# Moving the transposed activations out of the weight ring, with two changes to the start: one core, forgetting attention followed by spectral mixing

## The chip, the cores and the metric

The kernel runs on one core of one Trainium2 chip. The metric is the device time of one execution in microseconds (us), the median of several runs.

A word on two clocks. A run's reported time is 1.7 us longer than the span of the trace of that same run (489.44 against 487.7 us before the change). Times inside a trace count from the start of its span. "Mode" below means the matrix product for one Fourier mode; a "tile" is the 1 MB slot that holds the weights of four modes for one quarter of the input channels (0.5 MB real, 0.5 MB imaginary part, loaded as two DMAs).

In the profile lines PE is TensorE, PEld its weight loads, DVE VectorE, ACT ScalarE and POOL GpSimd; L83 is line 83 of that kernel, and `x6` means six instructions in one row.

## The reference, cut to what matters

```python
# q, k, v: (8, 8, 576, 64); f: (8, 8, 576); w_r, w_i: (64, 512, 512); w_ch: (512, 512)
attn = softmax(q @ k^T / 8 + cum[i] - cum[j], causal) ; x = attn @ v      # cum = cumsum(log f)
x = x.transpose(0, 2, 1, 3).reshape(8, 576, 512)
X = rfft(x, axis=1)[:, :64]
Y = einsum('bmd,mde->bme', X, w_r + 1j * w_i)          # 64 modes, 134 MB of float32 weights
y = irfft(Y, n=576, axis=1)
u = x + y
out = u + maximum(u @ w_ch, 0)
```

## The kernel before

The weights are cast to bfloat16 by the DMA on their way (67.64 MB landed through its queue, w_ch included, for 134 MB of float32) and stream through a ring of 9 slots. They are needed in order: 64 tiles, 16 for each quarter `dc` of the input channels. Attention runs in 32 steps (quarter by batch), and from step 9 on each step also does two tiles of modes for the quarter before it. When attention is over, 16 tiles are left; with them go the projections of x (`emit_xw`, which needs x^T) and of y (`emit_y`). A last stage adds all up and stores.

```python
    wpool = ctx.enter_context(tc.tile_pool(name="wpool", bufs=NRING))     # NRING = 9
    ...
    def emit_w_load(n):
        dc, g = tile_of(n)
        wb = wpool.tile([128, 2, MG, D], BF16, tag="wb", name="wb")
        for t, src in enumerate((moe_w_r, moe_w_i)):
            nc.gpsimd.dma_start(wb[:, t, :, :], ...)
    ...
        emit_basis()                  # Fourier basis, part of the setup
        emit_transposes(0)            # the first attention step's casts and transposes
        for s in range(NS + 1):
            ...
    # in emit_transposes(s):
            early = 5 <= s < B
            (nc.gpsimd if early else nc.vector).tensor_tensor(vb, v, wdec6, ALU.mult)
    ...
        XW = bsb.tile([128, B, NSB, D], BF16, name="XW")
        yy = bsb.tile([128, B, 2, D], BF16, name="yy")
    ...
            def emit_xw(b):
                xT = wpool.tile([128, NDC, SP], BF16, tag="wb", name="xT")   # a ring slot
                for eb in range(NDC):
                    ...                                   # 5 transposes into ptr
                    nc.vector.tensor_copy(xT[:, eb, :], ptr[:, :])
                for sb in range(NSB):
                    ...                                   # 4 matmuls with wch into pxw
                    nc.scalar.copy(XW[:, b, sb, :], pxw[:, :])
            ...
            while nmode < last:
                emit_modes(nmode)
                nmode += 1
                if nmode <= last - GL:                    # last = 64, GL = 4
                    if nx < B:
                        emit_xw(nx)
                        nx += 1
                    next_w()
                ...                                       # emit_y between the last four tiles
```

The order on each engine is not the order of this text: a scheduler decides it when the program is built.

The softmax here doesn't subtract the row's maximum and nothing guards it: scores larger than these inputs give would overflow.

## Time and profile before

| | before |
|---|---|
| time, median of 3 runs | 487.81 us (487.59 to 488.44) |
| HBM traffic | 163.73 MB read, 9.44 MB written |
| TensorE / VectorE / ScalarE / GpSimd busy | 68% / 52% / 51% / 27% of the span |
| first mode matmul | 89.7 us |
| projections of x | 381.1 to 428.0 us |
| end of the last mode, last stage | 444.4 us, then 43.3 us |

Four rows of the page's 40 slices (12.2 us each; busy tenths, TensorE's granted clock in tenths, GB/s moved), and the head of the chain that ended last, as shares of the span. This chain is the last instruction, followed back at each step to what it had waited for; a q marks an engine's sequencer, and "issue" is time without a visible cause:

```profile
PE   0668477899548566565566677763322899998994
PEclk9979789999875657766755677885555699989999
DMA  8999999999999999999999999999999999630577
GB/s 206 268 268 264 235 262 268 216 261 264 261 243 210 232 235 235 235 235 235 235 235 226 234 207 207 206 206 207 206 206 206 207 206 159 96 54 1 194 301 282
DMA 54%; PE 22%; ACT 7%; issue 2%; DVE 2%; POOL 0%; POOLq 0%; ACTq 0%; DVEq 0%
```

DMA is full for 33 slices and then fades (159, 96, 54 GB/s), while TensorE, which had idled (3, 3, 2, 2), is suddenly full. The two have changed places: first TensorE waits for weights, then weights wait for TensorE. GpSimd's timeline, which holds the weight issues, says why (start, duration, and in brackets the idle time before and what ended it):

```profile
399.58 0.74 POOL L83 DMA_DIRECT2D wb<-in_moe_w_r_dram  x1 [9.60 <-PE ptr L558]
400.31 0.76 POOL L83 DMA_DIRECT2D wb<-in_moe_w_i_dram  x1
410.65 0.74 POOL L83 DMA_DIRECT2D wb<-in_moe_w_r_dram  x1 [9.59 <-PE ptr L558]
411.38 0.75 POOL L83 DMA_DIRECT2D wb<-in_moe_w_i_dram  x1
422.39 0.74 POOL L83 DMA_DIRECT2D wb<-in_moe_w_r_dram  x1 [10.26 <-PE A L102]
```

Until 384 us a tile was issued every 5.1 us; here one in 11 us, after waits of some 10 us for the transposes (`ptr`): the slot that the load needs comes free only when TensorE gets on. The stretches of time show both sides, and an earlier hole. Each line has the stretch and its length, then the busy us (and number of instructions) of PE, PEld, DVE, ACT and POOL, then TensorE's clock, the busy share of DMA (1.24 is full when only weights move) and GB/s:

```profile
90.00:92.00 2.00, 1.97 (x58) 1.89 (x57) 2.00 (x7) 2.00 (x3) 0.16 (x1) 1.00 0.56 159
92.00:94.00 2.00, 1.75 (x47) 1.39 (x44) 1.42 (x6) 2.00 (x5) 1.41 (x3) 1.00 0.61 163
...
350.00:370.00 20.00, 4.75 (x128) 4.03 (x128) 2.43 (x4) 0.00 (x0) 5.92 (x8) 0.50 1.24 206
370.00:390.00 20.00, 11.37 (x109) 6.09 (x110) 4.29 (x10) 2.83 (x5) 5.92 (x8) 0.59 1.24 207
...
415.00:420.00 5.00, 5.00 (x40) 2.71 (x38) 1.69 (x4) 2.51 (x5) 0.00 (x0) 1.00 0.78 129
420.00:425.00 5.00, 4.99 (x65) 3.08 (x64) 2.21 (x5) 1.50 (x4) 1.48 (x2) 1.00 0.23 21
425.00:430.00 5.00, 5.00 (x100) 3.46 (x99) 1.01 (x2) 2.82 (x5) 0.00 (x0) 1.00 1.17 191
```

At 350 to 370 us TensorE works 4.75 of 20 us at half clock; at 420 to 425 us DMA runs at 0.23 where 1.24 is full. The hole at 90 us is the moment when the ring's first nine tiles had landed and no slot was free yet: no part of a weight load lands between 89.3 and 96.5 us.

In the start, one wait of TensorE stands out in its timeline:

```profile
58.68 0.66 PE L367 MATMUL tp<-ident_bf,vb 96*128 96x96 bf16 x6 [5.70 <-POOL vb L358]
```

GpSimd's scaling of v for steps 5 to 7 stands in its queue behind weight issues that wait for earlier loads, and TensorE stands still for 5.7 us.

### The profile page before, as it was taken

The numbers are of one execution on the slowest core, as the hardware profiler recorded it, in microseconds if no ns is written. First come the engines' busy times: TensorE is split into PE (matmuls) and PEld (weight loads), VectorE is DVE, ScalarE is ACT, GpSimd is POOL, SyncE is SP. The second block draws the span as 40 slices with busy tenths as digits, with TensorE's granted clock in tenths as the row PEclk, the third lists the DMA queues.
The fourth block names the chain that finished last, engine by engine and source line by source line (L and its number), as shares of the span: only waits on it lengthen the run. The fifth ranks groups of instructions, "written<-read, shape, count | busy, mean of one in ns | idle before, by whom it ended". The sixth has DMA issues, their size and how long they took to land.

```text
span 487.7 us, 11410 instructions
## 1 busy us (share of the span) xinstructions
PE 329.6 (68%) x4842; PEld 238.2 (49%) x4842; DVE 251.6 (52%) x618; ACT 250.0 (51%) x372; POOL 130.1 (27%) x157
## 2 busy tenths in 40 slices
PE   0668477899548566565566677763322899998994
PEld 0456355778446454454454555552311455565441
DVE  4858388898544444444444456552010322345874
ACT  2769589999545444444444556540000255434663
POOL 6111400241122122222221233223223311100795
PEclk9979789999875657766755677885555699989999
DMA  8999999999999999999999999999999999630577
GB/s 206 268 268 264 235 262 268 216 261 264 261 243 210 232 235 235 235 235 235 235 235 226 234 207 207 206 206 207 206 206 206 207 206 159 96 54 1 194 301 282
DMA packets 93203, 106.27 MB, mean 218 GB/s; under 512 B 4000, under 2 KB 88480, under 8 KB 93152
## 3 DMA queue, kind: packets, MB, share of 16 engines
q0 software_dynamic: 68112, 67.64, 83.4%
q1 hardware_dynamic: 25040, 37.90, 24.2%
q8 instruction: 38, 0.62, 0.5%
q14 instruction: 13, 0.11, 0.1%
HBM read 163.73 MB, written 9.44 MB: 355 GB/s over the span
## 4 chain that ended last, share of the span: by engine, by line
DMA 54%; PE 22%; ACT 7%; issue 2%; DVE 2%; POOL 0%; POOLq 0%; ACTq 0%; DVEq 0%
DMA wb<-in_moe_w_i_dram 42%; DMA wb<-in_moe_w_r_dram 12%; PE pxw L567 8%; PE A L102 2%; ACT E_129 L429 2%; PE pu L658 2%; PE pyw L579 2%; PE ptr L558 2%; PE pz L662 2%; PE pz L666 1%; ACT E_128 L429 1%; PE ps L422 1%; PE tp L367 1%; PE pav L456 1%; PE pu L654 1%
## 5 line engine op out<-in xcount | busy, mean ns | idle before, releaser
L102 PEld LDWEIGHTS <-wb 128*128 128x128 bf16 x2048 | 68.3, 101 | 123.4 <-DMA wb<-in_moe_w_i_dram 98.0
L83 POOL DMA_DIRECT2D wb<-in_moe_w_r_dram x64 | 47.7, 745 | 213.7 <-DMA wb<-in_moe_w_r_dram 92.9
L83 POOL DMA_DIRECT2D wb<-in_moe_w_i_dram x64 | 47.7, 746 | 105.4 <-DMA wb<-in_moe_w_i_dram 105.4
L429 ACT ACTIVATE E_129<-ps 128x1024 bf16<-128x1024 f32 x64 | 54.4, 869 | 15.2 <-PE ps L422 13.2
L429 ACT ACTIVATE E_128<-ps 128x1024 bf16<-128x1024 f32 x64 | 54.2, 871 | 6.8 <-PE ps L422 6.3
L574 ACT CAST XW<-pxw 128x512 bf16<-128x512 f32 x40 | 22.6, 586 | 66.9 <-PE pxw L567 66.9
L102 PE MATMUL A<-XT_1366,wb 128*128 128x16 bf16 x512 | 21.5, 175 | 38.0 <-DMA wb<-in_moe_w_i_dram 33.9
L113 DVE TENSOR_TENSOR Yacc<-A,Yacc 128x256 f32<-128x256 f32 x32 | 14.1, 441 | 62.9 <-PE A L102 62.2
L102 PE MATMUL A<-XT_2871,wb 128*128 128x16 bf16 x512 | 20.4, 174 | 29.8 <-DMA wb<-in_moe_w_i_dram 27.8
L567 PE MATMUL pxw<-wch,xT 128*128 128x512 bf16 x160 | 39.3, 400 | 0.0
L677 POOL TENSOR_TENSOR uo<-uo 128x1024 f32<-128x1024 f32 (+1 forms) x16 | 28.6, 1810 | 30.7 <-ACT uo L676 27.9
L102 PE MATMUL A<-XT_4376,wb 128*128 128x16 bf16 x512 | 16.4, 172 | 28.1 <-DMA wb<-in_moe_w_i_dram 17.7
L465 DVE TENSOR_TENSOR x_all<-pav,rcp 128x384 bf16<-128x384 f32 x64 | 31.1, 486 | 0.5
L422 PE MATMUL ps<-QTs,KTz_0_124 128*128 128x512 bf16 (+2 forms) x96 | 28.0, 337 | 2.7 <-ACT E_129 L429 1.7
L376 ACT COPY KTz_0_124<-tp 64x576 bf16<-64x576 bf16 x16 | 10.7, 667 | 36.6 <-PE tp L367 36.6
L422 PE MATMUL ps<-QTs,KTz_0_126 128*128 128x512 bf16 (+2 forms) x96 | 27.0, 337 | 3.6 <-ACT E_128 L429 2.2
L117 DVE TENSOR_TENSOR YT<-A,Yacc 128x256 bf16<-128x256 f32 x12 | 7.3, 611 | 42.0 <-PE A L102 42.0
L456 PE MATMUL pav<-va,E_128 128*128 128x65 bf16 x480 | 27.6, 217 | 1.4 <-DVE va L402 1.3
L376 ACT COPY KTz_0_126<-tp 64x576 bf16<-64x576 bf16 x16 | 10.9, 679 | 34.4 <-PE tp L367 34.4
L456 PEld LDWEIGHTS <-E_128 128*128 128x128 bf16 x480 | 25.0, 115 | 6.3 <-issue 4.6
L102 PE MATMUL A<-XT_453,wb 128*128 128x16 bf16 x512 | 18.8, 171 | 13.6 <-DMA wb<-in_moe_w_i_dram 11.1
L456 PE MATMUL pav<-va,E_129 128*128 128x65 bf16 x480 | 27.1, 215 | 0.1
(142 smaller groups left out, 776.7 us busy)
## 6 DMA issues: line engine op xcount, KB each, us to landing
wb<-in_moe_w_r_dram POOLq DMA_DIRECT2D x64, 512.0 KB, 22.9
wb<-in_moe_w_i_dram POOLq DMA_DIRECT2D x64, 512.0 KB, 23.8
out_dram<-uo SPq DMA_DIRECT2D x16, 512.0 KB, 3.6
stq_113<-in_q_dram SPq DMA_DIRECT2D x11, 288.0 KB, 6.4
stk_114<-in_k_dram SPq DMA_DIRECT2D x11, 288.0 KB, 7.1
stv_115<-in_v_dram SPq DMA_DIRECT2D x11, 288.0 KB, 7.7
stq_116<-in_q_dram SPq DMA_DIRECT2D x11, 288.0 KB, 7.7
stk_117<-in_k_dram SPq DMA_DIRECT2D x11, 288.0 KB, 6.7
```

The lines of the kernel that those rows point to most:

```text
L83: nc.gpsimd.dma_start(wb[:, t, :, :], src[g * MG : (g + 1) * MG, dc * 128 : (dc + 1) * 128, :].rearrange("m p e -> p m e"),)
L102: nc.tensor.matmul(A[:, eb, mi, :], lhsT=wb[:, t, mi, eb * 128 : (eb + 1) * 128], rhs=XT3[:, m, c0 : c0 + 2 * B], start=(t == 0), stop=(t ...
L113: nc.vector.tensor_tensor(ysl, A[:, :, :, :], ysl, ALU.add)
L376: nc.scalar.copy(KTz[s % NK][h][hs, 0:S].rearrange("c (p r) -> c p r", r=NR), tv[hs, :, :],)
L422: nc.tensor.matmul(ps[:, h, o : o + n], lhsT=KTz[s % NK][h][:, jb * 128 : (jb + 1) * 128], rhs=QT[s][:, jb * 128 + c0 : jb * 128 + c0 + n] ...
L429: nc.scalar.activation(E[:, :, piece * 512 : piece * 512 + w], ps[:, :, 0:w], ACT.Exp, scale=scale,)
L456: nc.tensor.matmul(pav[:, i, h, :], lhsT=E[:, h, c : c + 128], rhs=va[:, jb, h, :], start=(jb == 0), stop=(jb == sb),)
L465: nc.vector.tensor_tensor(x_all[:, b, sbs[0] : sbs[0] + n, dc * 128 : (dc + 1) * 128].rearrange("p c (h d) -> p c h d", h=2), pav[:, 0:n, ...
L558: nc.tensor.transpose(ptr[:, sc * 128 : (sc + 1) * 128], x_all[:, b, sc, eb * 128 : (eb + 1) * 128], ident_bf[:, :],)
L567: nc.tensor.matmul(pxw[:, :], lhsT=xT[:, eb, sb * 128 : (sb + 1) * 128], rhs=wch[:, eb, :], start=(eb == 0), stop=(eb == NDC - 1),)
L574: nc.scalar.copy(XW[:, b, sb, :], pxw[:, :])
L677: nc.gpsimd.tensor_tensor(o_sb, o_sb, u_sb, ALU.add)
```

## The change

The intent: x^T no longer takes slots from the weight ring but lies in the memory of `yy`, which is written only after the projections are done (three buffers in turn). The scaling of v is always on VectorE, so that it never stands behind weight issues. A scheduling barrier (no semaphore, only an order) keeps the first attention step's casts out of the setup.

```diff
-            early = 5 <= s < B
...
-            (nc.gpsimd if early else nc.vector).tensor_tensor(
+            nc.vector.tensor_tensor(
...
         emit_basis()
+        tc.no_sync_barrier()
         emit_transposes(0)
...
+        yflat = yy[:, :, :, :].rearrange("p b t e -> p (b t e)")
+        xTs = [
+            yflat[:, i * NDC * SP : (i + 1) * NDC * SP].rearrange(
+                "p (e s) -> p e s", e=NDC
+            )
+            for i in range(3)
+        ]
...
-                xT = wpool.tile([128, NDC, SP], BF16, tag="wb", name="xT")
+                xT = xTs[b % 3]
```

## The prediction

> **What bounds the kernel now.** The weight stream, then TensorE. The slices show DMA at 9 until 402 us, at 206 GB/s once only weights move. The chain of waits is 54% DMA (weight loads) and 22% PE; its TensorE part begins at 381.2 us: x^T projections back to back, 5.54 us each (20 transposes 1.12 us, 20 matmuls 4.42 us), until 428 us, then modes and y to 444.4 us. The last stage then runs 43.3 us.
>
> **The fault aimed at.** Each x^T takes one of the 9 weight slots. GpSimd's timeline shows weight issues every 5.1 us until 383.7 us, then only at 388.5, 399.6, 410.7 and 422.4 us: three wait 4 to 10 us for "PE ptr", that is for a slot. The stretches of time show DMA falling from 1.24 to 0.78 (415 to 420 us) and 0.23 (420 to 425 us). The last weight packet ends at 430.3 us; at 205.3 GB/s the bytes left at 400 us would have ended at 420.5 us. Meanwhile TensorE idles (4.75 us busy of 20 at 350 to 370 us), because in the built order 193 mode matmuls stand before the first projection.
>
> **What the change does.** In the changed kernel's built order TensorE takes one mode tile (32 matmuls), then one projection, eight times; then five tiles, six y, a tile, two y, two tiles. The work is only moved: about 44 us of projections go under the weight loads at 345 to 400 us. Per tile TensorE needs 0.85 + 5.54 = 6.4 us against 5.1 us of loading, so it falls behind by some 10 us, less than the ring's slack, and catches up after the eighth, near 400 us. y (1.09 us each) fits between the last tiles' arrivals. Modes should then end 1 us after the last weights land instead of 14 us.
>
> **Start.** VectorE waits 5.1 us for the second q load in the middle of the basis work; the fence puts the casts after it, so the first step starts some 4 us earlier. GpSimd's scaling of v (1.48 us each against 0.93 on VectorE) stands behind queued weight issues; this stops TensorE for 5.7 us at 53 to 59 us. Both go: modes should start near 80 us, not 89.6. But weights and q, k, v share the 16 DMA engines (weights drop from 206 to about 110 GB/s while q, k, v load), and those are already full. So most of these 10 us buys nothing; only the hole at 90 to 98 us (DMA share 0.56 and 0.61 at its low) closes: about 2 us.
>
> **Sum.** Last weights near 418.3 us (420.5 less 2.2), last mode 419.2, last stage 43.3: 462.5 us; plus 1 us for a colder TensorE clock. [...]clock 0.50 at 350 to 370 us, first projection 7.0 us instead of 4.42.
>
> Predicted 463.5 us, 8 in 10 between 459 and 469. Chances: faster by over 2% 0.96, within 2% 0.03, slower 0.01.
>
> **What would show it.** Weight issues keep 5.1 us spacing to the last, near 400 us; DMA full to 418 us; TensorE above 90% busy at 345 to 395 us at clock near 1.0; no TensorE wait for a GpSimd vb; no hole near 90 us; last stage still 43 us; almost no projections in the chain.
>
> **What would make it wrong.** A lowered clock during the projections (attention ran at 0.66), so that the ring stalls; VectorE, in order, holding x^T copies behind mode sums; or more empty DMA time in the start than the one hole.

(What is cut is a general rule about the clock, which this case does not show as such. No term of the sum is cut: 420.5 - 2.2 = 418.3, 0.9 more for the last mode is 419.2, with 43.3 it is 462.5, and with 1 for the clock 463.5 us. The 1 us is my estimate, a guess beside the measured values that follow the cut.)

## The result

| | before | after |
|---|---|---|
| time, median | 488.12 us (4 runs) | 470.27 us (470.05 to 471.23, 4 runs) |
| ratio | | 0.9638, 95% interval 0.9619 to 0.9656 |
| first mode matmul | 89.7 us | 78.9 us |
| projections of x | 381.1 to 428.0 us | 346.7 to 398.7 us |
| last weight load complete | 430.6 us | 422.4 us |
| last stage | 43.3 us | 46.1 us |

(A ratio is the mean time of one kernel's fast runs over that of the other's of the same rounds, so it is not quite the ratio of the medians quoted. The times of the last three rows are from the traces.)

The change gains 17.9 us where 24.6 were forecast, and 470.27 us lies above the forecast range. First what went as expected. The rows of the page after the change:

```profile
PE   1777778994676555766665666675379999588994
PEclk9978999997656667677757758787559999795998
DMA  8999999999999999999999999999999999970587
GB/s 204 269 267 268 268 268 267 268 267 254 225 236 236 236 236 232 230 232 234 231 230 235 236 227 205 207 206 207 206 207 206 207 207 207 206 120 1 203 325 278
DMA 76%; PE 10%; ACT 7%; issue 3%; DVE 2%; SPq 1%; POOL 0%; POOLq 0%; DVEq 0%; ACTq 0%
```

By the GB/s row DMA now stays full for two slices more and then stops, and the chain is DMA for 76% of the span. TensorE's full block begins some 35 us earlier (projections from 346.7 instead of 381.1 us), under the loads. The issues keep their pace to the last one:

```profile
397.26 0.74 POOL L83 DMA_DIRECT2D wb<-in_moe_w_i_dram  x1 [1.53 <-DMA wb<-in_moe_w_i_dram]
400.68 0.74 POOL L83 DMA_DIRECT2D wb<-in_moe_w_r_dram  x1 [2.68 <-PE A L102]
402.32 0.74 POOL L83 DMA_DIRECT2D wb<-in_moe_w_i_dram  x1 [0.90 <-DMA wb<-in_moe_w_i_dram]
```

The stretches that answer to those of before:

```profile
90.00:92.00 2.00, 1.68 (x36) 1.22 (x33) 2.00 (x4) 1.95 (x4) 0.00 (x0) 1.00 1.18 273
92.00:94.00 2.00, 1.94 (x52) 1.79 (x49) 1.74 (x7) 2.00 (x4) 0.74 (x1) 1.00 1.14 262
...
350.00:370.00 20.00, 19.98 (x218) 11.58 (x217) 6.62 (x15) 8.54 (x16) 5.92 (x8) 0.99 1.24 207
370.00:390.00 20.00, 19.98 (x220) 11.53 (x218) 6.62 (x15) 8.79 (x17) 5.33 (x8) 1.00 1.24 206
...
412.00:414.00 2.00, 2.00 (x17) 1.06 (x15) 0.85 (x2) 1.12 (x2) 0.00 (x0) 1.00 1.24 206
414.00:416.00 2.00, 2.00 (x17) 1.15 (x16) 0.85 (x2) 1.17 (x2) 0.00 (x0) 1.00 0.96 162
416.00:418.00 2.00, 2.00 (x43) 1.43 (x41) 1.03 (x2) 0.58 (x1) 0.00 (x0) 1.00 0.68 111
418.00:420.00 2.00, 2.00 (x41) 1.53 (x40) 0.85 (x2) 1.17 (x2) 0.00 (x0) 1.00 0.51 84
420.00:422.00 2.00, 0.27 (x11) 0.17 (x7) 0.61 (x1) 0.00 (x0) 0.00 (x0) 0.98 0.13 22
```

The hole at 90 us is closed. TensorE is busy 19.98 of 20 us at full clock where it had idled. No wait for a GpSimd `vb` is left. But the lower five lines show the first surprise. The stream does not stop at once: from 414 us DMA falls by steps, 162, 111, 84, 22 GB/s, over 8 us. The modes of a tile wait for its last byte: here it lands at 422.36 us, and they start at 422.40 us.

The second surprise is in the last stage. Three of its first matmuls in TensorE's timeline, before the change and after it:

```profile
447.65 0.38 PE L662 MATMUL pz<-XW,ident_bf 128*128 128x512 bf16 x1
447.87 0.38 PE L666 MATMUL pz<-yy,BI 128*128 128x512 bf16 x1
448.08 0.38 PE L658 MATMUL pu<-yy,BI 128*128 128x512 bf16 x1
```

```profile
427.93 0.63 PE L670 MATMUL pz<-XW,ident_bf 128*128 128x512 bf16 x1
428.36 0.64 PE L674 MATMUL pz<-yy,BI 128*128 128x512 bf16 x1
428.78 0.64 PE L666 MATMUL pu<-yy,BI 128*128 128x512 bf16 x1
```

Read the starts: 0.22 us apart before, 0.43 us after. The array runs at half clock, and does so until 432 us.

### Where the 16 parts of a load land

The trace records 16 landings for every weight load; they are called its 16 parts here. The modes start with the last one (landed at 422.36 us, start at 422.40). The page counts 16 DMA engines, but the trace does not say which engine a part belongs to: where the expectations speak of an engine, what is shown is a part. Worked out from those records, the times of the last load after the change, counted from its first part:

```
first part 414.65 us
+0.00 0.21 0.37 0.38 0.47 1.25 2.20 2.97 | 4.68 4.72 5.13 5.33 5.95 6.25 6.26 7.71
mean 418.02 us, last part 422.36 us
```

The mean, 418.0, is what the forecast took as the end of the stream (418.3). The last part comes 4.3 us after it. In the kernel before, the last load had waited for its slot until the queue was empty, and its 16 parts landed within 0.7 us; but the loads in the middle of that stream, too, were spread over 6.1 us (around 380 us in its trace). So what differs between the two ends is whether the queue had run dry; E9 asks whether the parts drift apart by themselves.

### The profile page after: what moved, and what is told of

The parts are those of the page before. It is cut to its first block, busy times and chain, and to the rows that moved or that the text cites. A ratio compares the mean times of both kernels' runs of the same rounds, so it can differ in the third digit from the quotient of the medians.

```text
span 469.5 us, 11440 instructions
## 1 busy us (share of the span) xinstructions
PE 333.5 (71%) x4842; PEld 239.1 (51%) x4842; DVE 252.0 (54%) x621; ACT 250.1 (53%) x372; POOL 125.5 (27%) x154
## 4 chain that ended last, share of the span: by engine, by line
DMA 76%; PE 10%; ACT 7%; issue 3%; DVE 2%; SPq 1%; POOL 0%; POOLq 0%; DVEq 0%; ACTq 0%
DMA wb<-in_moe_w_i_dram 70%; DMA stv_121<-in_v_dram 3%; DMA stk_117<-in_k_dram 2%; PE pu L666 2%; ACT E_128 L428 2%; PE pz L670 2%; PE pz L674 2%; ACT E_129 L428 1%; PE ps L421 1%; PE pu L662 1%; PE A L102 1%; PE tp L366 1%; ACT kb L351 1%; ACT KTz_0_124 L375 1%; PE pl L634 1%
## 5 line engine op out<-in xcount | busy, mean ns | idle before, releaser
L102 PE MATMUL A<-XT_1367,wb 128*128 128x16 bf16 x512 | 21.2, 174 | 40.1 <-DMA wb<-in_moe_w_i_dram 33.5
L102 PE MATMUL A<-XT_2872,wb 128*128 128x16 bf16 x512 | 20.2, 174 | 30.0 <-DMA wb<-in_moe_w_i_dram 28.3
L575 PE MATMUL pxw<-wch,yy 128*128 128x512 bf16 x160 | 38.9, 394 | 0.0
L421 PE MATMUL ps<-QTs,KTz_0_124 128*128 128x512 bf16 (+2 forms) x96 | 28.0, 346 | 2.9 <-ACT E_129 L428 1.8
L102 PE MATMUL A<-XT_454,wb 128*128 128x16 bf16 x512 | 18.6, 173 | 15.6 <-DMA wb<-in_moe_w_i_dram 14.4
L455 PEld LDWEIGHTS <-E_129 128*128 128x128 bf16 x480 | 26.0, 119 | 4.3 <-issue 3.4
L421 PE MATMUL ps<-QTs,KTz_0_126 128*128 128x512 bf16 (+2 forms) x96 | 25.9, 326 | 2.3 <-ACT E_128 L428 1.9
L455 PEld LDWEIGHTS <-E_128 128*128 128x128 bf16 x480 | 23.2, 112 | 7.6 <-DVE x_all L464 2.2
```

Of the source, the lines that this page charges most:

```text
L102: nc.tensor.matmul(A[:, eb, mi, :], lhsT=wb[:, t, mi, eb * 128 : (eb + 1) * 128], rhs=XT3[:, m, c0 : c0 + 2 * B], start=(t == 0), stop=(t ...
L421: nc.tensor.matmul(ps[:, h, o : o + n], lhsT=KTz[s % NK][h][:, jb * 128 : (jb + 1) * 128], rhs=QT[s][:, jb * 128 + c0 : jb * 128 + c0 + n] ...
L455: nc.tensor.matmul(pav[:, i, h, :], lhsT=E[:, h, c : c + 128], rhs=va[:, jb, h, :], start=(jb == 0), stop=(jb == sb),)
L575: nc.tensor.matmul(pxw[:, :], lhsT=xT[:, eb, sb * 128 : (sb + 1) * 128], rhs=wch[:, eb, :], start=(eb == 0), stop=(eb == NDC - 1),)
```

## The experiments

The theory after the first look: the time is that of the weight stream, plus its slowest part, plus a last stage that starts cold. What has to be tested: that the start's 10 us buy only the closed hole; that the half clock costs the last stage its 2.8 us; and what spreads the parts.

### E1: x^T alone

```diff
-        tc.no_sync_barrier()
+            early = 5 <= s < B
-            nc.vector.tensor_tensor(      # scaling of v
+            (nc.gpsimd if early else nc.vector).tensor_tensor(
```
(on the changed kernel: fence and v scaling put back as before)

> x^T in the space of y alone; fence and v scaling as before. Theory (the gain is made at the end of the weight stream; the start only closes the one hole near 90 us): the hole stays, the mean landing of the last load comes some 2.5 us later than in the changed kernel (418.0), the last of its 16 parts near 425 us, total 472.5 us (471 to 475). Rival (the 10 us gained at the start carry through): 478 us or more. Also: the last load's 16 parts land spread over 6 us or more, as in the changed kernel, since the queue never runs dry.

Measured: 473.03 us, ratio to before 0.9699 (0.9667 to 0.9730). The mean landing of the last load is at 421.2 us, its last part at 424.4 us, spread 5.7 us. First mode at 89.9 us, and the hole is there:

```profile
90.00:92.00 2.00, 1.96 (x59) 1.82 (x57) 2.00 (x7) 1.98 (x4) 0.00 (x0) 1.00 0.54 158
92.00:94.00 2.00, 1.70 (x49) 1.41 (x47) 1.42 (x7) 2.00 (x4) 1.55 (x2) 1.00 0.56 158
```

What follows: x^T alone makes about 14.5 us of the gain. Modes that begin 11 us later cost only some 3 us, the theory's share for the hole; the rival (478 us) is out.

### E2, E3, E4: the changes to the start, each alone and together, x^T in ring slots

```diff
# E2 fence only                 # E3 v only
+        tc.no_sync_barrier()   -  (nc.gpsimd if early else nc.vector).tensor_tensor(
                                +  nc.vector.tensor_tensor(
# E4: both
```

> The fence alone, x^T in ring slots. Theory: first step some 5 us earlier, modes begin near 85 us instead of 89.6, just before the ring would run empty, so the hole closes and the stream gains 2 to 2.7 us; the projections after it move with it: 485.3 us (484.5 to 487). Rival 1 (start is worth what it saves on the engines): 483 us. Rival 2 (the tail is paced by TensorE whatever the stream does): 487.8 us.

> v scaled on VectorE only, no fence, x^T in ring slots. Theory: the 5.7 us TensorE stall at 53 us goes, modes begin near 84 us, the hole closes just as with the fence alone, so this alone is worth as much as fence and v together: 485.3 us (484.5 to 487). Rival: each has its own part and this one gives nothing near 90 us: 487.8.

> Fence and v scaling together, x^T in ring slots. Theory: modes begin near 80 us, 9 us earlier, but the DMA engines were full apart from the hole: 485.0 us (484 to 487), no more than e2 or e3 alone. Rival (parts add up): e2 and e3 gains added, or 478 us if the 9 us at the start carry through.

| | time, us | ratio to before (95%) | first mode, us | stream's end by bytes left, us |
|---|---|---|---|---|
| before | 487.42 | | 89.7 | 420.5 |
| E2 fence | 485.40 | 0.9956 (0.9925 to 0.9987) | 88.6 | 419.4 |
| E3 v on VectorE | 483.22 | 0.9917 (0.9883 to 0.9951) | 80.8 | 417.6 |
| E4 both | 485.30 | 0.9952 (0.9923 to 0.9981) | 77.6 | 417.4 |

(Last column: bytes of weights still to come at 400 us, by the packet records, over 205.3 GB/s. Times of one call; the times of before varied by 4.6 us in it.)

What follows: E4 began its modes 12 us earlier than before and gained 2 us, so the start is worth the hole and not more. The parts do not add up: together they are no faster than the better one alone. E2 shows why the fence alone does little. Its first step begins at 14.8 instead of 20.0 us, but v still waits for the same weight issues in GpSimd's queue: TensorE's wait for `vb` grows from 5.7 to 9.6 us, and the first mode comes 1.1 us earlier only. So my expectation for E2 (modes near 85 us) was a miss, though the time came as expected; in E3 the modes began 3 us earlier than expected, and the time was 1.3 us below the range. Why E3 came out 2 us ahead of E4 is open: their streams end alike (417.6 and 417.4), the intervals overlap, and the difference arises in the projections and modes after 377 us.

### E5 and E8: TensorE kept busy before the last stage

```diff
             while nmode < last:
+                if nmode == last - 1:
+                    warm(10)             # 10 matmuls 128x512 into PSUM, never read
                 emit_modes(nmode)
 ...
+            warm(3)                      # after the loop
```
(E8: the same without the fence)

> The changed kernel with 10 unread 128x512 matmuls on TensorE ahead of the last weight tile's modes (2.1 us in which it otherwise waits for the load) and 3 ahead of the last stage. Theory (the last stage grew from 43.3 to 46.1 us because TensorE entered it at half clock; its matmuls took 0.43 us each until 432 us): they take 0.22 us from the start, last mode to end is 43.0 to 44 us, the last load lands as before at 422.4, total 467.8 us (467 to 469). Rival (the last stage grew for another reason, the clock is only a symptom off its critical path): 470.3 us, last stage 46 us.

> e5 without the fence: x^T in the space of y and v on VectorE, and the warming matmuls. Theory (with v on VectorE the fence adds nothing, since the modes then start before the ring runs dry anyway): the time of e5 within 1 us, mean landing near 418, no hole near 90 us. Rival (each of the two start changes has its own share): 2 us slower than e5.

Measured: E5 467.44 us (467.30 to 467.94), ratio 0.9571 (0.9547 to 0.9596); E8 467.40 us, ratio 0.9573 (0.9546 to 0.9600). From the start of the last mode's addition to the end of the span it is 43.4 us in E5 (422.38 to 465.8) and 43.4 us in E8, against 46.1 us in the changed kernel (423.44 to 469.5), 46.1 in E1 and 43.3 in the kernel before. (The last load landed at 421.4 us in E5, 1.0 us before its expected time; this is not part of the 43.4 us.) The matmuls of the last stage in E5:

```profile
426.18 0.38 PE L677 MATMUL pu<-yy,BI 128*128 128x512 bf16 x1
426.40 0.38 PE L681 MATMUL pz<-XW,ident_bf 128*128 128x512 bf16 x1
426.61 0.38 PE L685 MATMUL pz<-yy,BI 128*128 128x512 bf16 x1
```

What follows: 0.22 us apart again, and the last stage is back at its old length but for 0.1 us. The clock was the cause of 2.7 of the 2.8 us. The trace of the changed kernel shows when it fell. TensorE stood still from 420.3 to 422.4 us for the last load, and three of the stretches of that time give a clock of 0.95, 0.50 and 0.98:

```profile
421.00:422.00 1.00, 0.00 (x0) 0.00 (x0) 0.00 (x0) 0.00 (x0) 0.00 (x0) 0.95 0.08 13
422.00:424.00 2.00, 1.00 (x31) 0.91 (x31) 0.56 (x1) 0.00 (x0) 0.00 (x0) 0.50 0.00 0
432.00:436.00 4.00, 4.00 (x22) 1.89 (x21) 2.19 (x3) 2.60 (x3) 3.03 (x2) 0.98 0.33 129
```

From 424 to 432 us it is 0.50 too. Worked out from these shares, as an estimate, the half clock lasted from 421.9 to 432.2 us. It came when TensorE had stood still for only 1.6 us, and it lasted for some 4.6 us after the last pause, in which TensorE had waited once more, 1.1 us for ScalarE, until 427.55 us. What sets these lengths is not shown. E8 equals E5 (467.40 and 467.44 us): with v on VectorE the fence adds nothing that these runs show. Both are faster than the kernel before and the changed one; the gain over the latter is 0.9571 against 0.9638 of the same base, from different rounds.

### E6 and E7: fewer and more instructions

```diff
-                for t, c0 in ((0, B), (1, 0)):
+                # E6, dc < 3: only t = 1 (wrong on purpose);  E7, dc < 3: t = 0 twice (right)
```

> The changed kernel with only the second of each two mode matmuls in the first three quarters of the weights; wrong results on purpose. Weights, q, k, v and the end of the program are the same; 768 matmuls and their weight loads, some 98 KB of instructions, 6 of the 38 fetches of 16 KB, fall away. Theory (each instruction fetch puts one of the 16 DMA engines about 1 us behind the others, it stays behind while the queue never runs dry, and a load is complete only with the slowest): spread of the last load's 16 parts below the 7.7 us of the changed kernel, some 5 to 7, its mean landing about 0.4 us earlier than 418.0, last part 419.5 to 422, total 467.5 to 470. Rival (the spread comes from the engines themselves or from q, k, v): spread 7.7, last part 422.4, total 470.3.

> The reverse of e6: the first mode matmul of each pair done twice in the first three quarters (right results), 768 more matmuls and weight loads, 6 more fetches of 16 KB. Theory: spread 7.7 to 10 us, mean landing about 0.4 us later than 418.0, last part 422.5 to 425, total 470.5 to 473. Rival: as in e6, 7.7 us, 422.4 us and 470.3 us. Which engine a fetch falls on is not known, so a single run of this could miss.

| | fetches of 16 KB | spread of last load, us | mean landing, us | last part, us | time, us |
|---|---|---|---|---|---|
| E6 | 32 | 6.1 | 417.9 | 421.0 | 469.60 |
| after | 38 | 7.7 | 418.0 | 422.4 | 470.27 |
| E5 | 38 | 6.5 | 418.2 | 421.4 | (467.44) |
| E8 | 38 | 6.2 | 417.9 | 420.9 | (467.40) |
| E7 | 44 | 7.6 | 418.6 | 422.7 | 471.39 |

What follows: by the times and the last parts the order is right, but E5 and E8, with as many fetches as the changed kernel, spread nearly as little as E6, and E7's spread is no larger than the changed kernel's, just below its expected range. Runs with the same 38 fetches differ by 1.5 us, so a step of six fetches was too small; E6 and E7 settle nothing. (E6 was marked correct by the comparison's tolerance although its modes lack a term; nothing here rests on that.)

### E9 and E10: the stream by itself, without and with instructions

```diff
-    attention, projections, last stage: all left out; wrong on purpose
+    for n in range(64):
+        wb = wtiles.pop(n)
+        for i in range(NMM):             # E9: 2, E10: 76 small matmuls for each tile
+            nc.tensor.matmul(A[...], lhsT=wb[...], rhs=XT[:, :], start=True, stop=True)
+        nc.vector.tensor_copy(keep[:, :], A[:, 0, :])
+        if n + NRING < 64: emit_w_load(n + NRING)
```

> The 64 weight loads alone through the same ring of 9 slots, two small matmuls per tile so that a slot comes free, then the output filled with zeros; wrong on purpose. The queue never runs dry for some 327 us (67.1 MB at 205 GB/s). Almost no instructions, so 1 to 3 fetches of 16 KB in place of 38. Theory (an instruction fetch sets one DMA engine back by 1 us, and nothing evens it out): spread of the 16 parts stays at 0.5 to 1.5 us to the last load, last part about 0.5 us after the mean. Rival (the engines are unequal or drift by themselves): the spread grows to 4 us or more, as in the full kernel.

> The same with 76 small matmuls per tile, 4864 in all as in the full kernel, so again some 38 fetches of 16 KB; wrong on purpose; no q, k, v. Theory: the spread grows in steps of about 1 us, each beside a fetch, to 4 to 8 us at the last load, whose last part lands 2 to 5 us after the mean; the mean itself about 2.3 us later than in e9 (38 fetches of 0.95 us over 16 engines). Rival: as in e9, whatever that is.

"Fetches" are the packets of the page's DMA queues of kind `instruction`: 38 of 16 KB in the kernel before, in the changed one and in E10 (0.88 to 1.18 us each in the first two), besides smaller ones of up to 8 KB. Their number goes with the program: 32 of 16 KB in E6, 44 in E7. These two runs ask whether the weights pay for them. The same ring, the same 64 tiles, never dry. The 16 parts of the last load, from the landing records (E9's three fetches are one of 16 KB and two of 8 KB):

```
E9    3 fetches in the stream   0.00 0.02 0.04 0.05 0.07 0.09 0.10 0.19 0.31 0.33 0.34 0.35 0.49 0.50 0.75 1.19   mean 333.1, last 334.0 us
E10  38 fetches of 16 KB       0.00 0.04 0.09 0.23 0.25 0.26 0.64 0.88 4.56 4.60 4.70 5.56 5.69 5.73 5.78 5.81   mean 335.9, last 338.9 us
spread of E10's loads by landing time:  16 us 0.4, 24 us 1.3, 92 us 2.8, 164 us 3.6, 231 us 4.9, 306 us 5.8
fetches near those steps, us:           21.8 | 89.8 | 161.3, 163.8 | 229.0 | 300.9
```

The ends of the two streams in stretches, E9 first, then E10 (PE, PEld, DVE and POOL only; ScalarE has no work here):

```profile
330.00:332.00 2.00, 0.00 (x0) 0.00 (x0) 0.00 (x0) 0.00 (x0) 1.00 1.24 206
332.00:334.00 2.00, 0.00 (x0) 0.00 (x0) 0.00 (x0) 0.00 (x0) 1.00 0.47 77
```

```profile
330.00:332.00 2.00, 0.91 (x35) 0.81 (x31) 0.17 (x1) 0.00 (x0) 1.00 1.25 207
332.00:334.00 2.00, 0.23 (x8) 0.24 (x9) 0.00 (x0) 0.00 (x0) 1.00 0.94 158
334.00:336.00 2.00, 1.96 (x74) 1.87 (x71) 0.00 (x0) 0.00 (x0) 1.00 0.61 99
336.00:338.00 2.00, 0.00 (x0) 0.00 (x0) 0.17 (x1) 0.00 (x0) 1.00 0.55 91
338.00:340.00 2.00, 1.09 (x41) 1.10 (x42) 0.00 (x0) 0.00 (x0) 1.00 0.08 13
```

What follows: almost without instructions the stream ends sharply and its parts are within 1.2 us of each other after 334 us. With 38 fetches it ends in the long tail that the changed kernel has, and its last part lands 4.9 us later (338.9 against 334.0), where the mean moves by 2.8 us. The parts do not drift apart by themselves.

Are the fetches the cause, or the matmuls that they bring? The records settle it when E10 is followed load by load: 36 of its 38 fetches can be compared, by the last load that landed wholly before and the first that began to land after. At each of the 36, one part of the 16 falls back, by 0.7 to 1.4 us (mostly 1.1), and in 34 of them the other fifteen stay within 0.1 us. In the other two, another fetch lies between the two loads that are compared. From one fetch to the next nothing moves by more than 0.1 us, but for 0.25 us at an 8 KB fetch at 110 us, although the matmuls go on all the time. So the fetches make the steps. They take turns, too: after eight fetches, eight of the parts are 1.1 to 1.4 us behind the first one; after 16 the same number is 2.2 to 2.5 us behind, after 24 3.3 to 3.6 us, and the other eight never exceed 0.9 us. That is why the spread, set by the one slowest part, makes its larger steps at the 9th, 17th, 25th and 33rd fetch, the times above. Which DMA engines carry the fetches is not shown.

The same holds in the changed kernel once only weights move: across each of the 11 fetches from 291.7 to 403.4 us one part falls back by 0.85 to 1.14 us, and the others stay within 0.04 us, but for 0.3 to 0.5 us at three of them, beside an 8 KB fetch. Two of them hit the slowest part: the spread goes from 5.5 to 6.6 us at the fetch at 291.7 us, and at the one at 382.8 us from 6.63 us (load landing at 380.6 us) to 7.71 us (at 389.3 us), where it stays. Save for a load in flight at a fetch (8.27 us at 384.8 us), no part is seen to catch up in this kernel from 283 us on, nor in E10 from 20 us on; each keeps its delay from load to load. Before that the spread goes both ways (q, k and v load as well, until 276 us): it is 7.95 us at 202 us and 5.5 us at 283 us. How much of these 5.5 us came from fetches was not taken apart.

## Why the prediction was wrong, point by point

| step of the sum | predicted | measured (profiled run) |
|---|---|---|
| modes begin | near 80 us | 78.9 us |
| hole near 90 us closed, stream's bytes earlier by | 2.2 us | 2.8 us (420.5 to 417.7) |
| projections | 345 to 400 us, under the loads | 346.7 to 398.7 us |
| "Last weights near 418.3 us" | 418.3 us | mean 418.0, complete 422.4 us |
| "last mode 419.2" | 419.2 us | 423.4 us |
| "last stage 43.3 ... plus 1 us for a colder TensorE clock" | 44.3 us | 46.1 us |
| end | 463.5 us | span 469.5 us, median time 470.27 us |

The mechanism of the gain was right: where it is made, that TensorE follows one tile in 6.6 us and catches up, that the fence and the scaling of v pay only through the hole (E1 to E4). Two terms of the sum failed.

The first is "Last weights near 418.3 us". It was worked out as bytes left over rate, 420.5 less 2.2. That gives the mean of the 16 parts, and it was met to 0.3 us. The modes waited for the slowest part, and that was 4.3 us behind the mean. The trace of before hid it in the one place where I looked: there the last load ran alone in an empty queue and landed within 0.7 us. The loads that resemble the new end, those in the full stream, had 6.1 us of spread, and their landing records were there to be read. E9 and E10 show that the fetches of the program's instructions build such a spread in a stream of weights alone (5.8 against 1.2 us), one step of some 1.1 us on one part for each; in the changed kernel they added 2.2 of the 7.7 us after 283 us, and the share of fetches in the 5.5 us before is open. By removing the stall the change also removed the pause after which the parts had landed within 0.7 us, so part of the gain, some 4 us, was taken back in a new form.

The second is "plus 1 us for a colder TensorE clock". It was 2.8 us (46.1 against 43.3), and E5 shows that the clock is all of it but 0.1 us. The effect was foreseen, its size guessed; the profile of before had the number, as the first projection after idling took 7.0 us instead of 4.42, so 2.6 us, which I wrote down and did not use.

The two make 4.1 + 1.8 = 5.9 us of the 6.0 us between 463.5 and the span of 469.5. The rest is that I set a span in place of a time: reported times are 1.7 us above their span, and the profiled run after the change was 1.0 us slower than the median. 6.0 + 1.7 - 1.0 is 6.7 of the 6.8 us between 463.5 and 470.27.

That every expected sign in the profile save two came true (full DMA "to 418 us", last stage "still 43 us") is the lesson in reading: those two were the terms.

## What to carry to other kernels

When a load has to be waited for, do not take bytes over rate as its end: look at the landing of its slowest part (4.3 us behind the mean here) in the stretch that most resembles the new state, here the full stream and not the lone last load. A long unrolled program delayed the weight stream too, by its instruction fetches (some 1.1 us on one of the 16 parts for each 16 KB here), and a stream that never paused kept the delays (7.7 us of spread at its end). And when a change takes the work off TensorE just before a stage that it limits, try a few microseconds of unread matmuls in the gap: 13 of them were worth 2.7 us here.
